# Another order at the end of pass one, and the stores of pass two on ScalarE's queue, in a channel-attention kernel

## The chip, the cores and the metric

One core of one Trainium2 chip. The metric is the device time of one execution in microseconds (us). Every time below is the median of runs. What is read from a trace is one execution.

## The reference

```python
def reference(x, w1d):                      # x: (1, 384, 384, 384) bf16, w1d: (1,) bf16
    g = jnp.einsum("bhwc->bc", x) / (H * W) # mean of each channel over all pixels
    s = jax.nn.sigmoid(g * w1d[0])          # one factor per channel
    return x * s[:, None, None, :]
```

(Shortened to its case k = 1.) The input has 113 MB and must be read whole before the first output value is known. The core's memory holds only a part of it, so the rest is read twice, and 113 MB are written.

## The kernel before: the parts that matter

A row below is one row of 384 channels in each of the 128 partitions: 98304 B. There are 1152 rows. The *arena* holds some 270 of them.

Pass one streams all rows through the arena, and TensorE sums them with a matmul by ones. Some rows stay: 71 raw ones in the buffers U, V, A, Y and T, and groups that are *folded*: four rows are packed into the room of three by bit operations on VectorE. The small slots S1, S2, S3 are thirds of A. Pass two scales what is in the arena, stores it, and with the room that comes free loads the remaining rows again, scales and stores them. Folded rows are unfolded in between. One folded group is parked in PSUM, the memory of TensorE's results, and ScalarE copies it back in pass two.

All loads and stores are issued by SyncE ("SP"), in one queue:

```python
    def load(chunk, a, lo=0, hi=None):
        ...
        fl.add("SP", lambda: nc.sync.dma_start(out=arena[...], in_=view(xf, r0, n)[...]),
               writes=rows(a, hi - lo), dma=True)

    def store(chunk, a, lo, hi):
        ...
        return fl.add("SP", lambda: nc.sync.dma_start(out=view(of, r0, n)[...], in_=arena[...]),
                      reads=rows(a, hi - lo), dma=True)
```

`fl.add` derives the waits from the rows read and written. So a load waits until the store that emptied its rows has landed.

The order of pass two (which chunk VectorE works on, when a load goes, how big it is) is fixed at build time by a small model of the machine inside the kernel. Its model of the transfers matters later: `moves` is one line, and only its oldest entry is served.

```python
        while waiting and waiting[0][0] <= now:            # a store whose rows are scaled
            ...
            known.append(store(chunk, a, lo, lo + n))
            moves.append([now + LAT, n * ROW + PER_STORE, then])
        ...
                load(chunk, a)                             # a load into free rows
                ...
                moves.append([now + LAT, n * ROW + PER_LOAD, lambda parts=parts: landed.extend(parts)])
        ...
        if moves and moves[0][0] <= now:                   # the one line is served in order
            moves[0][1] -= DT
            if moves[0][1] <= 0:
                over.append((now + SEEN, moves.popleft()[2]))
```

## Time and profile before

| | before |
|---|---|
| time, median of the 3 runs at hand (range) | 723.07 us (722.98 to 723.43) |
| span of the profiled run | 721.2 us |
| bytes read and written | 190.41 and 113.25 MB |
| DMA rate over the span | 421 GB/s, 430 to 433 where full |
| VectorE busy | 496.2 us, 69% |

The lines that carry this are in the prediction. How to read them: DMA is full nearly everywhere, so time is bytes over rate plus the places where DMA is not full. One asks first for those places, and only then for the engines. In the lines by stretch, the last two figures are the DMA share (busy time of the 16 DMA engines; 1.00 is full) and the GB/s moved. Both can fall separately: at a full share and a low rate, the packets take longer for their bytes.

### The profile page before, as it was taken

The page shows a single profiled execution, that of the slowest core. Times are in us where ns is not written, and L with a number is a line of the kernel's source. Part 1 is how long each engine was busy: PE and PEld are TensorE (multiplying, and loading weights), DVE is VectorE, ACT ScalarE, POOL GpSimd, SP SyncE. Part 2 cuts the span into 40 slices and gives each one's busy share as a digit, 9 for nine tenths or more (in the row PEclk, how much of TensorE's full clock was granted, in tenths as well). Part 3 has the DMA queues.
Part 4 walks back from the last instruction along what each step waited for, and adds up shares of the span by engine and source line. Part 5 has one row for each costly group of instructions (what it writes and reads, how often), then busy time and mean ns, then how long its engine had stood idle before and what let it go on. Part 6 is the DMA issues. An engine that isn't in the chain of part 4 may idle for free.

```text
span 721.2 us, 3243 instructions
## 1 busy us (share of the span) xinstructions
PE 213.6 (30%) x1202; PEld 118.9 (16%) x1202; DVE 496.2 (69%) x469; ACT 115.4 (16%) x92; POOL 0.2 (0%) x4
## 2 busy tenths in 40 slices
PE   4677879889877780000000000000000000000000
PEld 2344445545444340000000000000000000000000
DVE  4600006887996729998999998999979994355330
ACT  3600004665774520000100000000000000000000
POOL 0000000000000000000000000000000000000000
PEclk9899999999999995555555555555555555555555
DMA  9999999999999988999999999999999999999997
GB/s 386 426 429 430 444 414 428 432 431 430 427 428 426 418 342 320 408 424 430 432 430 439 424 436 432 427 446 428 428 433 431 441 431 435 422 439 428 438 436 323
DMA packets 19890, 303.87 MB, mean 421 GB/s; under 512 B 2210, under 2 KB 2210, under 8 KB 6434
## 3 DMA queue, kind: packets, MB, share of 16 engines
q1 hardware_dynamic: 19872, 303.67, 98.7%
q8 instruction: 9, 0.15, 0.1%
q14 instruction: 7, 0.06, 0.0%
q10 hardware_dynamic: 2, 0.00, 0.0%
HBM read 190.41 MB, written 113.25 MB: 421 GB/s over the span
## 4 chain that ended last, share of the span: by engine, by line
DMA 56%; DVE 27%; PE 6%; another core or an unknown queue 4%; ACT 2%; SPq 1%; issue 0%; DVEq 0%
DMA arena<-in_x_dram 41%; DVE arena L433 18%; DMA out_dram<-arena 15%; DVE arena L251 6%; PE bank L227 6%; DVE arena L257 4%; ACT arena L291 2%; SPq L221 1%; ACT s_bf L424 0%; PE bank L505 0%; DVE odd L500 0%; DVE odd_i L509 0%; DVE worst L495 0%; DVEq L112 0%
## 5 line engine op out<-in xcount | busy, mean ns | idle before, releaser
L433 DVE TENSOR_TENSOR arena<-arena,s_bf 128x1536 bf16<-128x1536 bf16 (+8 forms) x102 | 241.8, 2411 | 71.8 <-DMA arena<-in_x_dram 57.5
L251 DVE TENSOR_SCALAR arena<-arena 128x1536 uint16<-128x1536 uint16 (+2 forms) x247 | 145.9, 634 | 111.6 <-DMA arena<-in_x_dram 100.8
L227 PE MATMUL bank<-arena,ones 128*128 128x384 bf16 x1152 | 205.4, 340 | 55.0 <-DMA arena<-in_x_dram 54.9
L227 PEld LDWEIGHTS bank<-arena,ones 128*128 128x128 bf16 x1152 | 114.0, 101 | 146.1 <-DMA arena<-in_x_dram 60.7
L257 DVE TENSOR_TENSOR arena<-arena 128x1536 uint16<-128x1536 uint16 (+2 forms) x114 | 121.0, 1062 | 10.3 <-PE bank L227 8.1
L291 ACT ACTIVATE arena<-arena 128x3072 uint16<-128x3072 uint16 (+1 forms) x38 | 102.5, 2696 | 146.1 <-DVE arena L251 146.1
L361 ACT COPY arena<-bank 128x512 uint32<-128x512 uint32 (+1 forms) x7 | 4.0, 571 | 70.5 <-DMA out_dram<-arena 70.3
L242 PE MATMUL bank<-ones,zeros 128*128 128x384 bf16 x48 | 8.3, 326 | 0.0
L291 ACT ACTIVATION_READ_ACCUMULATOR arena<-arena 128x1 f32 x38 | 7.1, 187 | 0.0
L242 PEld LDWEIGHTS bank<-ones,zeros 128*128 128x128 bf16 x48 | 4.7, 98 | 3.1
L505 PE MATMUL bank<-odd,ones 128*128 128x1 bf16 x1 | 0.2, 187 | 15.8 <-DVE odd L500 15.8
L361 ACT COPY bank<-arena 128x512 uint32<-128x512 uint32 (+1 forms) x7 | 3.6, 567 | 0.0
L505 PEld LDWEIGHTS bank<-odd,ones 128*128 128x128 bf16 x1 | 0.1, 106 | 16.2 <-DVE odd L500 16.2
L424 ACT ACTIVATE s_bf<-bank,w_sc 128x384 bf16<-128x384 f32 x1 | 0.6, 581 | 12.9 <-PE bank L227 12.9
L720 ACT ACT_TABLE_LOAD x1 | 1.3, 1283 | 0.7 <-PEq L736 0.7
L321 DVE TENSOR_SCALAR w_sc<-bank 128x1 f32<-128x1 f32 x1 | 0.2, 157 | 1.1 <-PE bank L316 1.1
L311 DVE MEMSET ones<- 128x128 bf16 x1 | 0.2, 165 | 1.0 <-SPq L106 1.0
L316 PE MATMUL bank<-w_bf,ones 1*128 1x1 bf16 x1 | 0.2, 181 | 2.1 <-DMA w_bf<-in_w1d_dram 2.1
L316 PEld LDWEIGHTS bank<-w_bf,ones 1*128 1x128 bf16 x1 | 0.1, 99 | 2.1 <-DMA w_bf<-in_w1d_dram 2.1
L509 DVE CAST odd_i<-bank 128x1 int32<-128x1 f32 x1 | 0.2, 158 | 0.3 <-PE bank L505 0.3
L495 DVE TENSOR_REDUCE worst<-seen 128x1 f32<-128x38 f32 x1 | 0.2, 182 | 0.0
L500 DVE TENSOR_SCALAR odd<-worst 128x1 bf16<-128x1 f32 x1 | 0.2, 156 | 0.0
(5 smaller groups left out, 0.5 us busy)
## 6 DMA issues: line engine op xcount, KB each, us to landing
arena<-in_x_dram SPq DMA_DIRECT2D x17, 4608.0 KB, 34.5
out_dram<-arena SPq DMA_DIRECT2D x6, 4608.0 KB, 43.9
arena<-in_x_dram SPq DMA_DIRECT2D x21, 1248.0 KB, 11.6
arena<-in_x_dram SPq DMA_DIRECT2D x9, 2304.0 KB, 27.3
out_dram<-arena SPq DMA_DIRECT2D x8, 2304.0 KB, 28.1
arena<-in_x_dram SPq DMA_DIRECT2D x4, 4512.0 KB, 33.6
out_dram<-arena SPq DMA_DIRECT2D x3, 4512.0 KB, 26.7
out_dram<-arena SPq DMA_DIRECT2D x9, 1248.0 KB, 12.0
```

The costliest lines, as they stand in the source:

```text
L221: lambda: nc.sync.dma_start(out=arena[:, a : a + hi - lo, :], in_=view(xf, r0, n)[:, lo:hi, :]),
L227: return nc.tensor.matmul(acc, lhsT=ones[:], rhs=arena[:, i, :], start=first, stop=last)
L242: lambda: nc.tensor.matmul(acc, lhsT=zeros[:], rhs=ones[:, None, :].to_broadcast([P, C // P, P]), start=False, stop=False),
L251: lambda: nc.vector.tensor_scalar(out=dst, in0=src, scalar1=s0, scalar2=s1, op0=op0, op1=op1),
L257: "DVE", lambda: nc.vector.tensor_tensor(out=dst, in0=a, in1=b, op=op), reads=reads, writes=writes
L291: lambda: nc.scalar.activation(out=y, in_=y, func=ACTF.Copy, accum_out=seen[:, 2 * k + i : 2 * k + i + 1]),
L316: lambda: nc.tensor.matmul(votes, lhsT=ones[0:1, :], rhs=w_bf[0:1, 0:1], start=True, stop=True),
L361: "ACT", lambda: nc.scalar.copy(dst.bitcast(u32), src.bitcast(u32)), reads=reads, writes=writes
L424: lambda: nc.scalar.activation(out=s_bf[:], in_=acc, func=ACTF.Sigmoid, scale=w_sc[:, 0:1]),
L433: lambda: nc.vector.tensor_tensor(out=v, in0=v, in1=s_bf[:, None, :].to_broadcast([P, n, C]), op=Op.mult),
L505: lambda: nc.tensor.matmul(votes, lhsT=ones[:], rhs=odd[:], start=True, stop=True),
L720: nc.scalar.preload_act_table(ACTF.Sigmoid)
```

## The change

Its intent, as the code shows it: (1) let the folds of the last two groups start earlier, and spread the uses of the small slots out, so that the end of pass one does not wait; (2) let loads of pass two go as soon as their rows are free, instead of behind a store that waits for VectorE.

```diff
     BETWEEN = [
-        ([], EARLY),
         ... (the middle entries change only their brackets)
-        (S1, S2, S3 + S1), (S2, S3, S1 + S2 + S3),
+        (S1, S2 + S3 + S1), (S2, S3 + S1),
     ]
     ...
             for e, f, where in zip(cuts, cuts[1:], blocks):
-                group_load(first three rows of the block); sum_rows(...)
-                stream_all(where)
-            group_load(fourth rows of the whole turn); sum_rows(...); fold(every piece)
-            stream_all(last)
+                group_load(g, 3 * e, 3 * f, ...); sum_rows(...)
+                if e == lo:
+                    group_load(g, 3 * q + lo, 3 * q + lo + n, beside); sum_rows(beside, n)
+                fold(the pieces of this block)
+                stream_all(where)
     ...
-    for a, n in SLOTS + [(V, 8), (U, 8), (Y, 8), (T, 5), (T + 5, 3)]:
+    for a, n in S2 + V1 + S3 + S1 + [(U, 8), (Y, 8), (T, 5), (T + 5, 3)]:
     ...
     def store(chunk, a, lo, hi):
-            "SP",
-            lambda: nc.sync.dma_start(...)
+            "ACT",
+            lambda: nc.scalar.dma_start(...)
```

(The calls in words stand for the lines of the original.)

More of the change, by code (lines that the diff above doesn't have):

```diff
@@ L377, in halves @@
         return [(a, n // 2), (a + n // 2, n - n // 2)]
+    V1 = [(V, 8)]
     EARLY = areas[1:5]
     BETWEEN = [
-        ([], EARLY),
-        ([], B3), ([], B4),
-        ([], B3), ([], AA),
-        ([], halves(areas[4])), ([], S1 + S2 + S3),
-        (S1, S2, S3 + S1), (S2, S3, S1 + S2 + S3),
+        (EARLY,),
+        (B3,), (B4,),
+        (B3,), (AA,),
+        (halves(areas[4]),), (S1 + S2 + S3,),
+        (S1, S2 + S3 + S1), (S2, S3 + S1),
     ]
     between = sum(n for b in BETWEEN[1:] for where in b for _, n in where)
+    first = N_STREAM - between
     at = 0
@@ L391 @@
             n = min(2 * PIECE, q - lo)
-            *blocks, last = BETWEEN[at]
-            cuts = [n * i // len(blocks) for i in range(len(blocks) + 1)]
+            beside = (U, V)[at % 2]
+            blocks = BETWEEN[at]
+            cuts = [lo + n * i // len(blocks) for i in range(len(blocks) + 1)]
             for e, f, where in zip(cuts, cuts[1:], blocks):
-                group_load(g, 3 * (lo + e), 3 * (lo + f), areas[g][0] + 3 * (lo + e))
-                sum_rows(areas[g][0] + 3 * (lo + e), 3 * (f - e))
-                stream_all(where)
-            beside = (U, V)[at % 2]
-            group_load(g, 3 * q + lo, 3 * q + lo + n, beside)
-            sum_rows(beside, n)
-            for k in of_group(g):
-                if lo <= pieces[k][1] < lo + n:
-                    fold(k, beside + pieces[k][1] - lo)
-            if g:
-                stream_all(last)
-            else:
-                first = N_STREAM - between
-                stream_all(EARLY[3:], first % 48)
-                stream_all(EARLY, first - first % 48)
-                folding = True
+                group_load(g, 3 * e, 3 * f, areas[g][0] + 3 * e)
+                sum_rows(areas[g][0] + 3 * e, 3 * (f - e))
+                if e == lo:
+                    group_load(g, 3 * q + lo, 3 * q + lo + n, beside)
+                    sum_rows(beside, n)
+                for k in of_group(g):
+                    if e <= pieces[k][1] < f:
+                        fold(k, beside + pieces[k][1] - lo)
+                if g:
+                    stream_all(where)
+                else:
+                    stream_all(EARLY[3:], first % 48)
+                    stream_all(EARLY, first - first % 48)
+                    folding = True
             at += 1
@@ L441, in store @@
         return fl.add(
-            "SP",
-            lambda: nc.sync.dma_start(out=view(of, r0, n)[:, lo:hi, :], in_=arena[:, a : a + hi - lo, :]),
+            "ACT",
+            lambda: nc.scalar.dma_start(out=view(of, r0, n)[:, lo:hi, :], in_=arena[:, a : a + hi - lo, :]),
             reads=rows(a, hi - lo), dma=True,
```

## The prediction

> **What bounds the kernel now.** I read the page first (busy shares, the slices, the chain), then busy time by stretch, then the waits of the issuing queue.
>
> The page's DMA lines:
>
> ```profile
> DMA  9999999999999988999999999999999999999997
> GB/s 386 426 429 430 444 414 428 432 431 430 427 428 426 418 342 320 408 424 430 432 430 439 424 436 432 427 446 428 428 433 431 441 431 435 422 439 428 438 436 323
> DMA packets 19890, 303.87 MB, mean 421 GB/s; under 512 B 2210, under 2 KB 2210, under 8 KB 6434
> q1 hardware_dynamic: 19872, 303.67, 98.7%
> ```
>
> The 16 DMA engines are full in every slice of 18 us but three: the two where pass one (sum all rows) hands over to pass two (scale and store), and the last. All data goes through one queue, that of SyncE. At the 430 GB/s of the full slices 303.87 MB take 707 us, of a span of 721.2. So the whole prize for keeping DMA fed is some 14 us, 2.0%, and part of it is start and end, which the change does not touch. I therefore look for the lost microseconds one by one (columns: stretch in us, its length, busy us of each engine, clock, DMA share, GB/s):
>
> ```profile
> 4.00:244.00 240.00, 191.72 (x1086) 107.66 (x1087) 125.22 (x173) 100.96 (x77) 0.00 (x0) 0.96 1.01 430
> 244.00:264.00 20.00, 15.38 (x82) 7.96 (x80) 12.98 (x18) 8.57 (x6) 0.00 (x0) 0.91 0.99 404
> 264.00:276.00 12.00, 6.10 (x36) 3.06 (x33) 4.82 (x4) 0.58 (x1) 0.00 (x0) 0.89 0.50 205
> 280.00:284.00 4.00, 0.00 (x0) 0.00 (x0) 4.00 (x3) 0.00 (x0) 0.00 (x0) 0.50 0.93 392
> 284.00:292.00 8.00, 0.19 (x1) 0.11 (x1) 7.65 (x12) 0.00 (x0) 0.00 (x0) 0.50 1.00 348
> 292.00:712.00 420.00, 0.00 (x0) 0.00 (x0) 337.11 (x258) 4.00 (x7) 0.00 (x0) 0.50 1.01 432
> 712.00:721.00 9.00, 0.00 (x0) 0.00 (x0) 0.00 (x0) 0.00 (x0) 0.00 (x0) 0.50 0.52 221
> ```
>
> Against 430 GB/s, the loss is length x (1 - rate/430): 244 to 264: 1.2 us. 264 to 276: 6.3. 280 to 284: 0.35. 284 to 292: 1.5. The end: 4.4. From 292 to 712, 420 us, nothing is lost on the whole. The first row (pass one) is as full.
>
> What happens in the 6.3 us gap is told by the chain of waits in time order:
>
> ```profile
> 257.70 10.02 DMA arena<-in_x_dram
> 267.71 0.05 issue
> 267.76 2.79 PE bank L227 x16
> 270.55 0.02 issue
> 270.57 0.59 ACT s_bf L424
> 271.16 0.02 issue
> 271.18 14.84 DVE arena L433 x8
> ```
>
> The last loads land, TensorE sums the last 16 rows, ScalarE makes the sigmoid, VectorE scales the first 4 rows (0.96 us), and only then can a store go. Nothing else can be moved meanwhile: the arena is full of rows that wait for the sigmoid.
>
> The waits of the issuing queue in pass two (engine, line, what for, total us, times, longest us):
>
> ```profile
> SPq L443 <- DVE arena L433: 267.3, 50, 29.7
> SPq L221 <- DMA out_dram<-arena: 114.6, 22, 16.3
> ```
>
> SyncE's queue spends 267 us standing before a store whose rows are not scaled yet. Loads written behind it stand too, even where their buffer is free. This looks like a large cost and is not one, because DMA stays full meanwhile. Pairing each issue with its landing, I count the rows under way when a DMA is issued: 21 to 62 rows (5 to 14 us at 0.229 us a row of 98304 B) from 284 to 331 us, then growing to 259 rows (59 us) at 620 us. Only the first stretch is shallow.
>
> **What the Trainium skill says.** (1) "DMA: Bandwidth & Descriptors", Issuing engines are not separate DMA queues: DMAs of SyncE and ScalarE run on the same 16 engines, so a second issuer saves sequencer time only. Here one store issue takes 0.33 us and 56 of them 18 us, hidden behind a full DMA. (2) The same page, Queues, rings and completion order: each engine takes turns between the queues that have work, packet by packet. This kernel has one busy queue, so its trace cannot show it. After the change a store will no longer stand behind every load issued earlier. (3) "Perfetto Trace Analysis", DMA Optimizations: one issuer for inputs and another for outputs allows "more dynamic spread". The 267 us above are the static order that this would loosen. (4) "HBM Reference", Specifications: a core streaming alone gets about 425 GB/s, bounded by its DMA engines. The trace agrees (430 and 432): pass two, with reads and writes in one queue, is at the same rate as pass one with reads only.
>
> **The change part by part.** The instructions of VectorE are the same in kind, size and order. TensorE sums the same 1152 rows. Bytes are equal.
>
> Part one, the order at the end of pass one. 26 rows move from small slots of 13 rows to the first big loads. At 208 to 244 us loads of 12 and 13 rows run at 420 to 434 GB/s, like the large ones, so this alone gains 0. Each of the last folded groups now gets its fourth rows right after its first 12, so folding starts earlier: 97 rows are loaded after the last 12 folded rows. Two folded pieces take 14.5 us before (243.05 to 257.6). The 97 rows take 22.2 us; the piece before lands 25 rows (5.7 us) earlier and takes 7.25 us, so the last fold starts 20.6 us before the last landing and ends 13 us before it, instead of 12 (257.6 against 269.5). That wait was hidden already: the loads of U, Y and T were issued with 42 to 55 rows ahead of them. Gain 0. What can count is the distance between two uses of one slot: before, the small loads cycle through three slots, and only 26 rows (5.9 us) are under way at each issue from 243.6 to 254.4. Just there the rate drops to 404. In the new order 34 to 58 rows lie between. If shallowness is the cause, up to 1.2 us comes back. I count 0.7.
>
> The last four loads (U 8 rows, Y 8, T 5, T 3) and the first things scaled (Y, T, U, V) are unchanged, so the gap keeps its 6.3 us.
>
> Part two, the stores on ScalarE's queue. The first eight stores come from VectorE at 0.2 us a row, so the first stores do not move. The first load of pass two needs the eight rows of V, whose store landed at 281.6. It was issued at 283.76, behind the seventh store. It can now go 2.1 us earlier, and fills the 0.35 us of 280 to 284. From 284 to 292 DMA is at share 1.00 but moves only 348 GB/s, with 21 to 34 rows ahead of each issue. If that too is shallowness, earlier loads give back part of the 1.5 us, and a little of 292 to 316 us, where the mean is 422 (another 0.4 us). I count 1.2 of these 2.25. After that DMA is full anyway: loads issued earlier land earlier, VectorE waits less, and nothing reaches the end.
>
> The end: 143 rows of stores are under way when the last one is issued at 692.3. So the last store still stands behind 27 us of DMA work, whichever queue it is on. Gain 0.
>
> Sum: 0.7 + 1.2 = 1.9, call it 2 us. 723.07 - 2 = **721.0 us**, 0.3% faster.
>
> **The rivals.**
> (a) The loosened order is worth much: the queue's 267 us and VectorE's 57.5 us of waiting for loads (9 waits) shrink and the end comes 10 us or more earlier, 713 or less. Against it: no lost DMA time from 292 to 712, and bytes are equal.
> (b) Two queues change the rate. Reads and writes then truly overlap in each engine, instead of blocks of 0.4 to 4.7 MB in turn. If HBM or the engines dislike it by 2%, 420 us become 428 and the time is 730. If they like it, 715. For it speaks only that this trace has no such mixture; against it, that 430 for reads and 432 for the alternation are so near each other.
> (c) A new wait takes the place of the old. ScalarE must copy the parked rows back from PSUM in the midst of the stores, after an earlier store has landed: before, it sat 70.3 us for that, harmlessly; now stores queue behind it. But the copies began when the 24-row store landed at 341.4, take 4.0 us, and the next store was not ready before 358.4. Also VectorE is 95% busy from 292 to 532 (228.16 of 240 us), so a load passed by stores could stall it. But while both queues have work, loads get half the turns, as they need. Loss 0, at worst 2 us.
> (d) Nothing at all: the low rates at 250 and 288 us are not shallowness, and only 0.35 us comes back: 722.7.
>
> **Range and chances.** Centre 721.0. The lower end 717.5 takes all of the 1.2 + 2.25 us (719.6) and a rate gain of 0.5% on 420 us. The upper end 723.8 is rival (d) with a small loss of rate or a wait of 1 us. 2% is 14.5 us, more than all idle DMA time, so faster by over 2% needs a rate that no stretch here shows: 0.02. Slower by over 2% needs 3.4% less rate through pass two, or a stall of DMA that now has 5 us of work in hand at its shallowest: 0.02. Within 2%: 0.96.
>
> **What would show it.** Right: 404 in the stretch before the handover rises towards 430; the gap of 6.3 us stays, with the same 16 rows on TensorE before the sigmoid; the first load of pass two goes out some 2 us earlier, and 280 to 292 carries more than 363 GB/s; the 267 us before stores move to ScalarE's queue; stores land sooner after issue; VectorE waits less for loads; pass two after that still runs at 432. Wrong: another mean rate in the long stretch (rival b), holes in it (c), or a shorter handover gap, which I don't see a reason for.

## The result and the profile after

| | before | after |
|---|---|---|
| time, median (range), 4 runs each | 723.03 us (722.71 to 723.43) | 726.59 us (725.62 to 727.21) |
| ratio | 1 | 1.0048 (95%: 1.003 to 1.0065) |
| span of the profiled run | 721.2 us | 725.3 us |

The change costs 3.6 us. The forecast was a gain of 2 us (717.5 to 723.8 us for the time).

The page of the changed kernel, the DMA lines:

```profile
GB/s 371 439 432 426 439 426 428 432 431 431 430 424 428 426 295 362 427 426 429 380 409 433 446 421 428 434 438 416 418 437 421 434 432 427 444 416 425 439 430 331
q1 hardware_dynamic: 11520, 190.42, 61.8%
q10 hardware_dynamic: 8066, 113.25, 36.7%
```

There are two data queues now, q1 with all loads and q10 with all stores, and bytes are as before. New is the slice with 380, the twentieth of the forty slices, at about 345 to 363 us: between the handover and the last slice, none was below 408 before. By stretch, in the changed kernel (columns as in the prediction):

```profile
244.00:264.00 20.00, 14.10 (x82) 7.39 (x81) 9.82 (x14) 8.21 (x6) 0.00 (x0) 1.00 1.01 425
284.00:292.00 8.00, 0.19 (x1) 0.10 (x1) 7.65 (x12) 0.00 (x0) 0.00 (x0) 0.50 1.00 385
292.00:712.00 420.00, 0.00 (x0) 0.00 (x0) 336.53 (x258) 4.00 (x7) 0.00 (x0) 0.50 1.00 427
...
350.00:375.00 25.00, 0.00 (x0) 0.00 (x0) 24.10 (x19) 0.00 (x0) 0.00 (x0) 0.50 0.96 383
375.00:712.00 337.00, 0.00 (x0) 0.00 (x0) 261.01 (x197) 0.00 (x0) 0.00 (x0) 0.50 1.01 430
```

The last two stretches ran at 432 and 433 GB/s before; the first of them:

```profile
350.00:375.00 25.00, 0.00 (x0) 0.00 (x0) 24.03 (x19) 0.00 (x0) 0.00 (x0) 0.50 1.01 432
```

In time: 25 x (1 - 383/432) = 2.8 us lost in one hole, and 337 x (1 - 430/433) = 2.3 us in small pieces after it. Pass one did what was forecast: 244 to 264 us went from 404 to 425 GB/s, and the sigmoid starts at 270.06 instead of 270.57 us. The chain of waits of the changed kernel shows the same handover after it:

```profile
267.25 2.79 PE bank L227 x16
270.04 0.02 issue
270.06 0.59 ACT s_bf L425
```

Who waits in pass two, first the queue of SyncE (now loads only), then VectorE:

```profile
SPq L221 <- DMA out_dram<-arena: 302.7, 26, 30.5
```

```profile
DVE arena L251 <- DMA out_dram<-arena: 26.9, 2, 20.7
DVE arena L434 <- DMA arena<-in_x_dram: 21.7, 7, 5.3
```

The 267 us before stores are gone from SyncE's queue, as intended, but its loads now wait 302.7 us for stores to land; it was 114.6. VectorE waits less for loads (57.5 us before), and twice, 26.9 us in all (4.4 before), for a store to land.

### The profile page after: what moved, and what is told of

It reads as the page before. It is cut to its first block, busy times and chain, and to the rows that moved or that the text cites. A ratio compares the mean times of both kernels' runs of the same rounds, so it can differ in the third digit from the quotient of the medians.

```text
span 725.3 us, 3253 instructions
## 1 busy us (share of the span) xinstructions
PE 212.6 (29%) x1202; PEld 118.6 (16%) x1202; DVE 496.1 (68%) x469; ACT 115.4 (16%) x92; POOL 0.2 (0%) x4
## 2 busy tenths in 40 slices
DMA packets 19602, 303.87 MB, mean 419 GB/s; under 512 B 2178, under 2 KB 2178, under 8 KB 6402
## 4 chain that ended last, share of the span: by engine, by line
DMA 50%; DVE 30%; PE 7%; another core or an unknown queue 3%; ACT 3%; SPq 0%; issue 0%; DVEq 0%
DMA arena<-in_x_dram 32%; DMA out_dram<-arena 18%; DVE arena L434 17%; DVE arena L251 7%; PE bank L227 7%; DVE arena L257 5%; ACT arena L291 3%; SPq L221 0%; DVEq L106 0%; ACT s_bf L425 0%; PE bank L506 0%; DVE odd L501 0%; DVE odd_i L510 0%; DVE worst L496 0%
## 5 line engine op out<-in xcount | busy, mean ns | idle before, releaser
L506 PE MATMUL bank<-odd,ones 128*128 128x1 bf16 x1 | 0.2, 187 | 15.8 <-DVE odd L501 15.8
## 6 DMA issues: line engine op xcount, KB each, us to landing
out_dram<-arena ACTq DMA_DIRECT2D x9, 1248.0 KB, 13.9
```

Source lines behind the costliest of these rows:

```text
L506: lambda: nc.tensor.matmul(votes, lhsT=ones[:], rhs=odd[:], start=True, stop=True),
```

## How one late store becomes a hole

The hole can be followed back step by step in the two traces. In each step I paired the issue with its landing.

| step | before | after |
|---|---|---|
| store of 13 rows: issued, landed | 310.0, 322.2 (12.2 us) | 309.5, 325.3 (15.8 us) |
| load of 13 rows into their place: issued, landed | 322.2, 335.9 | 325.3, 339.8 |
| VectorE, in its fixed order, starts to scale them | 335.96 | 339.80 |
| their store: issued, landed | 338.7, 352.3 (13.6 us) | 342.6, 360.4 (17.8 us) |
| the next load, of 26 rows, goes | 352.3 | 360.4 |

VectorE's line for it in the timeline, before and after (the brackets hold how long it was idle, and what ended that):

```profile
335.96 2.76 DVE L433 TENSOR_TENSOR arena<-arena,s_bf 128x4992 bf16<-128x4992 bf16 x1 [1.87 <-DMA arena<-in_x_dram]
```

```profile
339.80 2.76 DVE L434 TENSOR_TENSOR arena<-arena,s_bf 128x4992 bf16<-128x4992 bf16 x1 [5.25 <-DMA arena<-in_x_dram]
```

And the last store of the table, before and after (columns: count, issue in ns, first and last issue in us; then issue to landing):

```profile
L443 SPq DMA_DIRECT2D out_dram<-arena x1: 332/332/332, 338.7 to 338.7; - x1
DMA to landing us min/median/max: 13.6/13.6/13.6
```

```profile
L444 ACTq DMA_DIRECT2D out_dram<-arena x1: 338/338/338, 342.6 to 342.6; - x1
DMA to landing us min/median/max: 17.8/17.8/17.8
```

When this store was issued after the change, 18 rows of loads and 26 of stores were under way, 10 us of work, and 4 us later a load of 21 rows was issued. The load landed at 360.4, with the store, though it was issued behind it. In one queue it would have stood behind it. The load of 18 rows had passed this store already when it was issued: before, it went 2.7 us after the store (341.4 against 338.7), now 3.5 us ahead of it (339.1 against 342.6). Over the whole of pass two the passing can be counted: in the kernel before, all 82 transfers landed in the order of their issue; in the changed one (80 landings traced), 28 pairs landed in the opposite order, 27 of them a store passed by a load.

How the two queues share the engines shows in the packets (the pieces of a transfer) of 344 to 356 us of the changed kernel, q1 with loads, q10 with stores (packets, MB, share):

```profile
q1 hardware_dynamic: 223, 3.10, 61.7%
q10 hardware_dynamic: 224, 2.02, 39.6%
```

Each queue had half the packets, but not half the bytes. The packets of the loads (18 and 21 rows) were larger than those of the stores (13 and 8 rows), so the loads moved about 60% of the bytes. From 346.5 to 360.4 us nothing new was issued at all: the loads waited for this store, and VectorE was unfolding and scaling (busy 13.83 of these 13.9 us), with its next store not ready before 362.2. What was under way ran out. Before the change, the load of 26 rows had gone 8.0 us earlier and bridged it. The DMA at that place, after and before:

```profile
358.00:360.00 2.00, 0.00 (x0) 0.00 (x0) 2.00 (x3) 0.00 (x0) 0.00 (x0) 0.50 0.90 377
360.00:363.00 3.00, 0.00 (x0) 0.00 (x0) 3.00 (x2) 0.00 (x0) 0.00 (x0) 0.50 0.76 220
363.00:368.00 5.00, 0.00 (x0) 0.00 (x0) 5.00 (x4) 0.00 (x0) 0.00 (x0) 0.50 0.96 354
```

```profile
360.00:363.00 3.00, 0.00 (x0) 0.00 (x0) 2.10 (x3) 0.00 (x0) 0.00 (x0) 0.50 1.04 444
363.00:368.00 5.00, 0.00 (x0) 0.00 (x0) 4.97 (x4) 0.00 (x0) 0.00 (x0) 0.50 1.00 430
```

That is a reading of traces, not yet a proof.

## The experiments

Fourteen kernels, each timed in five rounds (five or six runs) beside the kernel before (722.88 to 723.14 us there). The theories at first: **A**, stores lose their place in the line, buffers come free late, VectorE stalls and DMA runs dry. **B**, two queues move fewer bytes at a full DMA share, whatever the order. **C**, ScalarE is a bad issuer, as its copies from PSUM stand between the stores.

### 1. The parts alone

The changed kernel with its stores back on SyncE's queue:

```diff
-            "ACT",
-            lambda: nc.scalar.dma_start(out=view(of, r0, n)[...], ...)
+            "SP",
+            lambda: nc.sync.dma_start(out=view(of, r0, n)[...], ...)
```

> Part one alone: the new order at the end of pass one, all stores on SyncE's queue again. All theories of the loss put it into pass two with two queues, so they expect this kernel to be at or a little under the kernel before: 722.0 to 722.8 us, with 244 to 264 us at about 425 GB/s as in the changed kernel (404 before) and no hole near 360 us. If instead the order is to blame, it is near 726.

Measured: 722.98 us (722.90 to 723.82), ratio 1.0001 (0.9988 to 1.0015). 244 to 264 us at 424 GB/s, no hole. Part one is worth nothing that shows; 722.98 is just above the 722.0 to 722.8 expected. The 0.5 us that its pass one ends earlier in the profile is inside the spread.

The kernel before with only the queue of the stores changed (the reverse of that edit):

> Part two alone: the old order of pass one, stores on ScalarE's queue. If two queues are the cause, in whichever way, it keeps the whole loss: 726 to 728 us, a hole in the DMA's rate between 350 and 375 us. If the loss needs both parts, it is near 723.

Measured: 726.76 us (725.91 to 728.23), ratio 1.0053 (1.0039 to 1.0067), with the hole:

```profile
350.00:375.00 25.00, 0.00 (x0) 0.00 (x0) 24.90 (x21) 0.00 (x0) 0.00 (x0) 0.50 0.96 384
```

So the whole loss is part two.

### 2. One queue, but ScalarE's; and two queues, exchanged

```diff
     def load(...):
+        by, eng = ("ACT", nc.scalar) if second else ("SP", nc.sync)     # second: in pass two
-        fl.add("SP", lambda: nc.sync.dma_start(...))
+        fl.add(by, lambda: eng.dma_start(...))
```

> The changed kernel with the loads of pass two on ScalarE's queue as well, so that one queue carries both again in the program's order. Theory A (stores lose their place: the engines take turns between two queues, loads issued later pass older stores, buffers come free late, VectorE waits and DMA runs dry near 360 us) and theory B (two queues at once move fewer bytes at a full DMA share) both expect 722 to 723 us and 432 GB/s after 292 us. Theory C (ScalarE as issuer: its copies from PSUM stand between the stores) expects the loss to stay: 725 us or more.

Measured: 723.85 us (723.18 to 724.15), ratio 1.001 (0.9996 to 1.0024). 350 to 375 us at 433 GB/s, 292 to 712 at 431. Theory C falls: ScalarE issues all of pass two, its copies stand in the same line, and the time, 0.8 us over that of before, is not apart from it (the interval holds 1).

The same, with the stores on SyncE's queue and the loads of pass two on ScalarE's:

> Two queues with the parts exchanged: loads of pass two on ScalarE's queue, stores on SyncE's, plan as in the changed kernel. Both theories of two queues expect 726 to 727.5 us, with the run-down near 360 us; if it mattered which engine issues the stores, it would differ by more than 1 us.

Measured: 726.33 us (725.98 to 727.55), ratio 1.0047 (1.0034 to 1.006). The time is as expected, the place is not: 350 to 375 us ran at 429 GB/s, and 414 to 474 us at 419 (437 before). Which queue carries which does not matter to the time; where the loss falls depends on details of timing. The trace shows the detail. Here the loads stand in ScalarE's line behind its copies from PSUM, which began at 339.25 us. So the load of 18 rows was issued at 343.0, after the store of 13 rows (341.8) and not before it. That store landed after 12.6 us, and the load of 26 rows went at 354.4. Where the store kept its place, the hole did not open, with two queues.

### 3. Is it VectorE, close to its limit?

Four of the six operations of `fields` in the unfolding were dropped, with wrong results (relative error 0.057). The plan, all transfers and their order stay.

```diff
         def fields():
             bits(u, w0, SHR, 4, AND, 0x0780, wc[0], uc)
-            bits(b, w1, SHR, 8, AND, 0x0078, wc[1], bc)
-            bits(c, w2, SHR, 12, AND, 0x0007, wc[2], cc)
-            join(u, u, b, OR, uc + bc, uc)
             bits(b, w2, SHL, 4, AND, 0x8000, wc[2], bc)
-            join(u, u, c, OR, uc + cc, uc)
```

> The changed kernel with four of the six operations that take the folded fourth row apart left out (a wrong result on purpose; bytes, issues and their order as before). VectorE then has some 85 us less to do in pass two and is no longer close to its limit. Theory A (late loads stall VectorE, and DMA runs dry behind it): the hole near 360 us closes, the time falls to about 722.5 us, within 1 us of the same kernel on one queue. Theory B (two queues move fewer bytes at full share): DMA is the bound in both, so it stays 3 us or more above that kernel.

> The same light kernel with its stores on SyncE's queue, the partner of the run before. It was bound by DMA already, so both theories expect 722 to 723 us. It serves as the zero for the light kernel with two queues.

Measured: 728.8 us (726.86 to 731.5) with two queues, 722.1 us (721.79 to 722.95) with one. VectorE was relieved by 49 us between 292 and 712 (287.26 against 336.53), not by 85 as I had estimated. The two-queue kernel got worse, not better: 6.7 us above its partner. It has a shallow dip at 350 to 375 us (407 GB/s) and a hole later:

```profile
422.00:442.00 20.00, 0.00 (x0) 0.00 (x0) 19.86 (x17) 0.00 (x0) 0.00 (x0) 0.50 0.94 364
```

Its partner on one queue ran that stretch at 442. This part of theory A fell: relieving VectorE over pass two does not close the hole. It does not show that VectorE is without a part in it, for in the hole itself VectorE was busy 19.86 of the 20 us. At 427.0 us, when a store was issued after 16.7 us without a new transfer, only 14 rows of stores and no load were under way, 3.2 us of work. What is common is that the work under way runs down. I call what is left of the theory A2: passed stores free their rows late, and the work under way runs out.

### 4. Where in pass two?

The first 21 stores (up to 344 us) on one engine's queue, the other 35 on the other's:

```diff
+        of_acts = len(stores) < 21        # or: >= 21, or: >= 36
+        stores.append(0)
-            "ACT", lambda: nc.scalar.dma_start(...)
+            "ACT" if of_acts else "SP",
+            lambda: (nc.scalar if of_acts else nc.sync).dma_start(...)
```

> The changed kernel with only the first 21 stores (up to about 344 us) on ScalarE's queue, the rest on SyncE's. Theory A: the shallow first stretch makes the hole, so it stays: 2.8 of the 3.6 us, about 725.5 us. Theory B: two queues last only 70 of 450 us, so a sixth of the loss: about 723.6 us.

Measured: 725.78 us (725.42 to 726.06), ratio 1.0043 (1.003 to 1.0056). 70 us of two queues make 2.9 of the 3.6 us, in the hole; after it the rate is that of before:

```profile
350.00:375.00 25.00, 0.00 (x0) 0.00 (x0) 24.90 (x20) 0.00 (x0) 0.00 (x0) 0.50 0.98 385
375.00:712.00 337.00, 0.00 (x0) 0.00 (x0) 259.35 (x196) 0.00 (x0) 0.00 (x0) 0.50 1.01 433
```

> The opposite: the first 21 stores on SyncE's queue, the later 35 on ScalarE's. Theory A: no hole near 360 us, what is left is what 375 to 712 us lost (430 against 433 GB/s, 2.3 us) less where deep queues forgive it: 723 to 725 us. Theory B: five sixths of the loss, about 726 us, with a rate of 427 to 430 GB/s spread over the whole stretch.

Measured: 726.88 us (726.63 to 727.51), ratio 1.006 (1.0047 to 1.0073), the number that theory B named. But the trace does not show B's even loss. It shows the hole again, 40 us later:

```profile
350.00:375.00 25.00, 0.00 (x0) 0.00 (x0) 17.51 (x15) 0.00 (x0) 0.00 (x0) 0.50 1.01 433
390.00:415.00 25.00, 0.00 (x0) 0.00 (x0) 24.90 (x23) 0.00 (x0) 0.00 (x0) 0.50 0.94 374
```

25 x (1 - 374/432) = 3.4 us. In both runs a hole opened soon after two queues began, in a stretch with little work under way. That left both A2 and B, so the next one starts two queues where much is under way (`len(stores) >= 36`).

> The changed kernel with only the last 20 stores (from about 490 us on, with 20 to 60 us of work in flight) on ScalarE's queue, the others on SyncE's. Theory A2: nothing to run out, 722.7 to 723.5 us. Theory B: some 230 of 450 us with two queues, half of the 3.6 us: 724.5 to 725 us.

Measured: 723.21 us (722.23 to 723.57), ratio 1.0003 (0.999 to 1.0016), with 432 GB/s from 375 to 712. From 460 to 670 us transfers of both queues were under way together for some 190 us. Transfers passed each other there too (23 pairs landed out of order), and it cost nothing. Theory B falls: two queues have no lower rate of themselves.

### 5. What does one run-down cost?

Part one alone, on one queue, and one load held back until everything before it has landed:

```diff
-                load(chunk, a)
+                load(chunk, a, after=newest[-1:] if todo - n < 400 <= todo else ())
```

(`newest` collects the stores in order; `after` adds the wait. On one queue everything behind this load waits too.)

> Part one alone, on one queue, with one load near 490 us held until the store issued last before it has landed, so that the DMA queue runs empty once. It measures what one run-down costs. If only the idle time counts: 2 to 2.5 us over part one alone (issue to first byte and landing to issue), 725.3 us. If a restart also runs at a low rate at full share for some 8 us, as after the sigmoid (348 GB/s), 726.5 to 727.5 us.

Measured: 728.55 us (726.65 to 729.59), 5.6 us above part one alone, more than either guess:

```profile
498.00:502.00 4.00, 0.00 (x0) 0.00 (x0) 3.97 (x7) 0.00 (x0) 0.00 (x0) 0.50 0.91 390
502.00:505.00 3.00, 0.00 (x0) 0.00 (x0) 3.00 (x4) 0.00 (x0) 0.00 (x0) 0.50 0.06 24
505.00:520.00 15.00, 0.00 (x0) 0.00 (x0) 13.35 (x15) 0.00 (x0) 0.00 (x0) 0.50 1.00 381
```

Against 430 GB/s: 0.4 us while it empties, 2.8 us empty, and 1.7 us after the restart, with the share at 1.00 and a rate of 381. Such a low rate at a nearly full share also stands after the hole of the changed kernel (354 GB/s at 0.96), and at 284 to 292 us in the kernel before (348 at 1.00). It does not follow every restart at once: from 276 to 280 us, just after the first stores, the kernel before ran at 429. The run-down was not made good later, and cost more than its empty microseconds.

### 6. Taking the passing away, with two queues

The closest test: two queues and the plan stay, but a load may pass at most two stores.

```diff
-                load(chunk, a)
+                load(chunk, a, after=newest[:-2])
```

> The changed kernel, with each load of pass two held until all stores planned before it, but the last two, have landed: two queues, but a load can pass at most two stores. Theory A2 (passing makes buffers come free late and the work in flight run out): the run-down near 360 us is gone, 722.5 to 724.5 us. Theory B (two queues cost of themselves): 726 us or more.

Measured: a median of 723.75 us, against 726.59 for the changed kernel. Four of six runs lie at 723.07 to 723.84, one at 725.62, one at 730.84; the ratio with all six is 1.0032 (1.0001 to 1.0063), which overlaps that of the changed kernel (1.003 to 1.0065). So the times alone do not settle it; why two runs were long is not known. The trace, of the run at 723.66 us, says more. The chain of the table above is back to its old times: the store of 13 rows is issued at 309.6 and lands after 11.9 us, its successor is issued at 338.9 and lands after 11.2 us, and the load of 26 rows goes at 350.1 us, 10.2 us earlier than in the changed kernel, although the load of 18 rows now goes 7.9 us later (347.0 against 339.1). The hole is gone:

```profile
350.00:375.00 25.00, 0.00 (x0) 0.00 (x0) 22.19 (x18) 0.00 (x0) 0.00 (x0) 0.50 1.02 435
375.00:712.00 337.00, 0.00 (x0) 0.00 (x0) 259.51 (x196) 0.00 (x0) 0.00 (x0) 0.50 1.00 430
```

An added wait took the hole away, and by the medians made the kernel 2.8 us faster. That is A2: **the plan was made for one line in order of issue. With two queues, loads pass stores; a passed store frees its rows late; the load that waits for these rows goes late, and with it VectorE, which keeps its order; and in the stretch with little work under way, DMA runs dry.** The small losses after 375 us (430 against 433) remain here and are not explained.

### 7. Making the plan for two queues: it did not help

If the plan no longer fits its queues, a plan that knows two queues should.

```diff
-        if moves and moves[0][0] <= now:
-            moves[0][1] -= DT
-            ...
+        heads = [next((m for m in moves if m[3] == q), None) for q in "SL"]   # oldest store, oldest load
+        live = [m for m in heads if m and m[0] <= now]
+        for m in live:
+            m[1] -= DT / len(live)
+            ...
```

> The changed kernel, with the planner of pass two taught about two queues: its model of the transfers now serves the oldest store and the oldest load at half the rate each while both wait, instead of one line in order of issue. Order of VectorE's work, sizes and buffers follow from it; bytes are the same. Theory A2 (the plan was made for one line; with two queues loads pass stores, buffers come free later than planned, and the work in flight runs out once): the run-down near 360 us disappears and the time comes back to 722 to 724 us. Theory B (two queues move fewer bytes, whatever the plan): 726 us or more.

> The plan for two queues, run with all stores and loads on SyncE's queue. Theory A2: a plan that doesn't fit its queues costs, here too: a run-down somewhere, 724 us or more. Theory B: one queue is what counts, 723 us.

> The plan for two queues with one of its thresholds moved (a load of 8 rows or more goes at once only if less than 7 us of work is ahead, not 9): 27 loads instead of 31, and no rest of one row. If the plan's small pieces and its tail ate the gain of the closed run-down: 723 to 725 us. If two queues cost of themselves: 726.5 us or more again.

| | time | 292 to 712 us |
|---|---|---|
| plan for two, two queues | 727.33 us (725.43 to 728.16) | 430 GB/s |
| plan for two, one queue | 725.94 us (725.26 to 726.77) | 372 to 400 us at 409 GB/s |
| plan for two, one threshold moved, two queues | 729.44 us (728.59 to 735.03) | 428 to 452 us at 398 GB/s |

One part came as expected: the plan for two has no hole at 350 to 375 us on two queues (427 GB/s). Run on one queue it was slower, as expected, but not by a run-down: the 409 GB/s came at a full share (1.01), and from 372 to 400 us at least 34 rows (8 us) were under way at each issue. And the time of the first did not come back (727.33 us is in the range that B gave), and the second attempt is the slowest of all. What the traces show: 1584 more packets (21186 against 19602), and a ragged end, where from 717 to 723 us DMA moves 113 GB/s at a share of 0.28 (301 at 0.71 in the kernel before with only the queue of the stores changed, whose span is the same). Also, the new model gives each queue half the rate, while the traces show half the packets each. Which of these made the plan for two a worse plan was not separated. The conclusion rests on the experiments of sections 4 and 6, not on this one.

No version with a correct result beat the kernel before.

## Why the prediction was wrong

**Right.** The bound (DMA, with no more than 14 us to win), the loss of 2% or a gain of 2% ruled out, and part one in its mechanism: 404 rose to 425 GB/s, the gap at the sigmoid stayed, and 0.5 us of the 0.7 foreseen showed in the profile's pass one, though not in the time (722.98 us alone).

**Wrong in size.** Of the 1.2 us that earlier loads were to give back, the first load did go 2.6 us earlier (281.1 against 283.8 us), but 276 to 292 us only rose from 379 to 384 GB/s: 0.2 us. The low rate stayed and moved along with the first loads: 280 to 284 us fell from 392 to 343, and 284 to 292 us rose from 348 to 385. That shallowness is its cause is not shown; the cause is open.

**The step that failed** is the sentence "After that DMA is full anyway: loads issued earlier land earlier, VectorE waits less, and nothing reaches the end", and with it rival (c)'s "while both queues have work, loads get half the turns, as they need. Loss 0, at worst 2 us". I asked only what the turns do to loads. And half the turns were not half the bytes (about 60% to the loads from 344 to 356 us). A store that is passed lands later, and in this kernel a store's landing is what releases the next load. The landing of one store went from 13.6 to 17.8 us, and the next load from 352.3 to 360.4. The forecast "stores land sooner after issue" failed with it: of the 54 stores traced in both kernels, 23 did. I had also called the 5 us of work under way a reserve that would hold. It was the plan's reserve, worked out for one line, and an order that loosens the line spends it. The hole did not even open in the stretch that I had counted as shallow (284 to 331 us), but at 358 to 368 us, where the kernel before had 47 rows or more (11 us) under way at each issue. Rival (b), a change of rate, was refuted by the late switch (723.21 us). Two slips in the prediction had no effect: its 259 rows under way include the one just issued (211 without, as in its other counts), and rival (b)'s 730 and 715 start from different times (about 721 and 723).

## What to carry to other kernels

A second issuing queue is not only a way to save issue time: it gives up the order between the two kinds of transfer, and here the kind with the larger packets got more of the bytes. Where a load waits for a store to free its buffer, let loads pass stores only where the work under way is deep, or hold them to their place with an explicit wait. And when a schedule is worked out ahead against a model of the machine, a change of queues changes the model, so look at how long single transfers take to land, not only at how full the engines are.

## What the Trainium skill lacked or had wrong

- "DMA: Bandwidth & Descriptors", Issuing engines are not separate DMA queues: it says that a second issuer only saves sequencer time. Here it changed which transfer is served first, and the kernel took 3.6 us of 723 longer. The section Queues, rings and completion order states the turn-taking, which agrees with the store passed here (17.8 against 13.6 us to land) and with the packets counted (223 and 224), but not this consequence, nor that equal turns can be unequal bytes (3.10 and 2.02 MB).
- "Perfetto Trace Analysis", DMA Optimizations: one issuer for inputs and another for outputs "may make sense", above all with loops or control flow, for "more dynamic spread". In this kernel, with a fixed plan, that is 0.5% slower (1.0048), and with queues exchanged too (1.0047). The page does not say when it hurts.
- No page has it: a nearly full DMA can move fewer bytes for a while (348 GB/s over 8 us where the loads of pass two come in, 381 over 15 us after a forced drain, where 430 is usual). Why is open.
- No page has it: one forced run-down in a DMA-bound stretch cost 5.6 us, of which DMA was empty for about 3.
- "HBM Reference", Specifications: about 425 GB/s for a core alone. The full stretches here ran a little above, at 430 to 433, for reads alone and for reads with writes.
